# One-plane key pooling, three buffers for the high and low parts, and a new order of work

## The chip, the core and the metric

The kernel runs on one NeuronCore of a Trainium2 chip. Five engines run side by side, each through its own instruction list in order: TensorE (PE, with its weight loads shown as PEld), VectorE (DVE), ScalarE (ACT), GpSimd (POOL) and SyncE (SP), which issues most of the DMA transfers. An instruction that waits holds back everything behind it on its engine. The DMA transfers of all of them run on the same 16 DMA engines. The metric is the time of one execution on the device, in microseconds (us), lower is better.

## What is computed

Attention over keys that are pooled in 4 x 4 blocks, and behind it a soft mixture of experts. q has 4 batches of 12,288 rows of 128; kv is 4 x 384 x 32 x 128, so pooling leaves 768 keys a batch, each the mean of 16 planes of kv.

```
kv_pool = kv.reshape(B, H // 4, 4, W // 4, 4, C).mean(axis=(2, 4))
k = v = kv_pool.reshape(B, -1, C) @ w_sr
s = (q @ k.T) / sqrt(C);  a = softmax(s, -1);  x = a @ v
logits = x @ phi                                   # 32 slots
d = softmax(logits, 0);  slot_input = d.T @ x
slot_out = per expert: relu(slot_input @ w1) @ w2   # 8 experts
out = softmax(logits, 1) @ slot_out
```

## The kernel before, in words

The rows of q are cut into 384 tiles of 128 rows, 96 a batch; 12 tiles make a group, 8 groups a batch, 32 in all. Attention is never written out: what leaves it are the logits of the second stage and running sums over the slots.

For a tile, PE multiplies q by the 768 keys in split precision (lines 388 to 390, six matmuls into `s`), DVE takes the row maximum (394, 395), ACT the exponential into `p` (403). Of each row of `p`, 384 columns are turned on DVE into `pa` (`ptr`, 427). The other 384 go another way: ACT writes their high half in 16 bits, two tiles at a time, into a buffer `hl` (`p_hi`, 410); POOL writes the low half beside it (`p_lo`, 414, one instruction a tile); and SP issues a DMA transpose of the tile from `hl` into `pb` (`p_dma`, 423). There are two `hl` buffers, so a conversion on ACT waits until both transposes of the pair two conversions back have landed. SP issues 384 such transposes, one a tile. SP also loads q for four tiles at a time (234), which ACT and POOL split (368, 372).

Behind every 12 tiles PE makes the group's logits from `pa` (459, `LA`) and `pb` (471, `LB`) in 96 and 36 matmuls; ACT and DVE evacuate one half each (480, 482), PE adds them up (488, `lsel`), DVE turns them into `LL` (497 to 500). A chain over POOL, DVE, PE and ACT (503 to 578) makes the weights `D` of the group, and PE multiplies them with the group's `p` tiles (588, `T`, a pair of tiles is one block of matmuls). POOL and ACT make the row-wise exponentials in `LL` for the last stage (604 to 610).

The pooled keys of the first batch are made on DVE. Those of the next three are pooled by DMA while the batch before runs: `plan_keys` puts a plain load of two planes on SP (257) and seven accumulating loads of two planes on POOL's queue (259), each waiting for the one before, and then one accumulating copy of the first plane onto the second (`kv_fold`, 263). They use idle slots of `LL`. At the switch to the next batch PE forms keys and values from the sum (`pk` 271, `pu` 286, `put` 315, `pv` 331), ACT and DVE evacuate them.

The last stage (the tail) loads w1 and w2 and the spilled `LL` rows (`pb<-spill`, 831), runs the experts (845 to 908), normalises the rows of `LL` on DVE and POOL (949 to 958), and then for each of the 32 groups turns, multiplies, evacuates and stores the result (976 to 995).

The order on PE, DVE, ACT and POOL is written out in advance: every operation gets a key, its place of origin plus an entry of the table `TAU` (raised above the keys of what it depends on), and all are emitted by rising key. SP's list is ordered by the framework.

Of the kernel before, what the change touches and what calls it, by code (L numbers as in the profile page):

```python
# [19 lines left out]
P = 128  # L20
# [35 lines left out]
    "lev0": 18.513, "lev1": 18.513, "crec11": 18.527, "reps": 18.807, "rinv": 18.974, "lsel": 19.037, "ltr": 19.601,  # L56
    "ln": 20.079, "csum19": 20.551, "csum25": 20.707, "mcol": 21.235, "mmm": 21.629, "mred": 22.122, "dsub": 22.358,
# [5 lines left out]
    "kv4": 39.365, "cmul27": 40.126, "bev": 40.196, "uhl": 42.368, "cexp": 43.449, "spill": 44.522, "wl4": 44.887,  # L63
# [32 lines left out]
def attention_then_soft_moe(ctx: ExitStack, tc: tile.TileContext, E, qT, kv0, kvT, w_sr, w_srT, phi, w1, w2, outT, spill):  # L96
# [14 lines left out]
    G = 12  # L111
# [3 lines left out]
    KVC = 2  # L115
    GH = G // 2
    NSL = 16
    NA = 3
# [15 lines left out]
        "s": 3, "T": 1, "x": 1, "p": 13, "pa": 3, "pb": 3, "hl": 2, "q": 3, "qs": 2, "lps": 1, "g": 3,  # L134
# [27 lines left out]
    def kvb(b):  # L162
        o = (b % 2) * (NSL // 2) * G * NS
        return flat[:, o : o + KVC * NK].rearrange("p (a n) -> p a n", a=KVC)

# [88 lines left out]
    def kv_acc(b, c):  # L254
        dst, src = kvb(b), kvT[b - 1, :, c * KVC : (c + 1) * KVC, :]
        if c == 0:
            nc.sync.dma_start(out=dst, in_=src)
        else:
            nc.gpsimd.dma_start(out=dst, in_=src, accum_op=ALU.add, max_dma_last_dim=4 * 2 * NK)

    def kv_fold(b):
        t = kvb(b)
        nc.gpsimd.dma_start(out=t[:, 1:, :], in_=t[:, :1, :], accum_op=ALU.add, max_dma_last_dim=4 * 2 * NK)
        PO[b] = t[:, 1, :]
# [281 lines left out]
    def d_sub(g):  # L546
        d = GD[g]
        d["D"] = ring(gp, "D", [P, G, NS], f"D_{g}", F32, "g")
        nc.gpsimd.tensor_tensor(  # L549
            out=d["D"], in0=lsl(g), in1=MRUN[g].unsqueeze(1).broadcast_to([P, G, NS]), op=ALU.subtract  # L550
        )
# [11 lines left out]
    def d_exp(g):  # L563
        d = GD[g]
        nc.scalar.activation(d["D"], d["D"], AF.Exp)
# [140 lines left out]
    def plan_logits(g):  # L706
# [16 lines left out]
        e1 = op("DVE", "lev1", at, [a], lambda: l_ev(g, 0), use=[sl[0]] + lk)  # L723
        mk = ("x", ("psl", g))
        a = op("PE", "lsel", at, [e0, e1, ops["us", b]], lambda: l_sel(g), acq=[mk], use=lk + [("K", b)])
        ops["lt", g] = op("DVE", "ltr", at, [a] + ([ops["vm", b]] if b and g % GPB == KVC else []), lambda: l_tr(g), acq=[("c", g)], use=[mk, ("g", g)])

    def plan_group(g):
        b = g // GPB
# [322 lines left out]
```

## Time and profile before

| | |
|---|---|
| three timed runs | 1022.58, 1026.76, 1033.25 us; median 1026.76 us |
| profiled execution | 1019.8 us, of which the span of the instructions is 1018.0 us |
| busy share of the span | PE 87%, DVE 77%, ACT 65%, POOL 63% |
| DMA engines | 67.7% for SP's and ACT's transfers, 10.3% for POOL's |
| mean granted TensorE clock | 0.946 of full speed |

Matmuls are pipelined, so a PE that is busy all the time is not necessarily at its peak; instructions that issue a DMA are not counted as busy. A wait is put down to what came last by the profile. In the views below, a stretch is given in us from the start of the span.

### The profile page before, as it was taken

To read this page: it belongs to the slowest core of one execution; us is meant where nothing else is said; L and a number is where in the kernel's file an instruction comes from. 1 tells how busy PE (TensorE), PEld (TensorE's weight loads), DVE (VectorE), ACT (ScalarE), POOL (GpSimd) and SP (SyncE) were. 2 spreads that over 40 slices of the span, in tenths; PEclk is the share of its full clock that TensorE was granted. 3 is DMA by queue.
4 is the path that set the end of the run, shared out by engine and by line. 5 is a ranking of instruction groups with operands and counts; after the bars stand their busy time and mean duration, and the time that the engine had idled before them with its cause. 6 is when DMAs were issued, how large, how long until landed. Compare 5 with 4: busy or idle time off the path is not lost. (4 is left out here: it accounts for less than half of the span.)

```text
span 1018.0 us, 27047 instructions
## 1 busy us (share of the span) xinstructions
PE 884.1 (87%) x10436; PEld 623.3 (61%) x10436; DVE 787.4 (77%) x1496; ACT 663.8 (65%) x1244; POOL 641.1 (63%) x774
## 2 busy tenths in 40 slices
PE   1878999989979999989889989999999999965673
PEld 0756666665756667766666667766777777632341
DVE  6757787877967779878777768978998989935765
ACT  1756767766766678767767758787887888710333
POOL 1556676776657668775766657776776777747300
PEclk9989998999999999999999989999999999987657
DMA  8597886897887898895889886976676676692788
GB/s 325 100 154 135 163 138 133 164 187 134 131 159 143 148 153 150 146 205 119 158 144 151 147 147 129 172 147 108 136 130 113 135 131 125 101 361 120 285 345 361
DMA packets 335264, 168.78 MB, mean 166 GB/s; under 512 B 310432, under 2 KB 312736, under 8 KB 335008
## 3 DMA queue, kind: packets, MB, share of 16 engines
q1 hardware_dynamic: 331248, 149.22, 67.7%
q0 software_dynamic: 3456, 17.70, 10.3%
q8 instruction: 82, 1.34, 0.6%
q14 instruction: 46, 0.38, 0.1%
q10 hardware_dynamic: 432, 0.15, 0.1%
HBM read 62.01 MB, written 28.31 MB: 89 GB/s over the span
## 5 line engine op out<-in xcount | busy, mean ns | idle before, releaser
L414 POOL TENSOR_TENSOR hl<-p,hl 128x384 f16<-128x384 f32 x384 | 349.5, 928 | 205.1 <-ACT hl L410 196.7
L394 DVE TENSOR_REDUCE nm<-s 128x1 f32<-128x768 f32 x384 | 363.3, 946 | 68.9 <-PE s L390 66.4
L403 ACT ACTIVATE p<-s,nm 128x768 f32<-128x768 f32 x384 | 344.0, 896 | 91.3 <-DVE nm L395 83.7
L388 PE MATMUL s<-khi,qhi 128*128 128x384 f32 x768 | 287.6, 374 | 21.8 <-ACT p L403 21.7
L389 PE MATMUL s<-klo,qhi 128*128 128x384 f32 x768 | 263.4, 343 | 2.1 <-DVE klo L278 2.1
L390 PE MATMUL s<-khi,qlo 128*128 128x384 f32 x768 | 263.8, 343 | 0.0
L410 ACT ACTIVATE hl<-p 128x768 f16<-128x768 f32 x192 | 161.2, 840 | 98.9 <-DMA pb<-hl 92.4
L388 PEld LDWEIGHTS s<-khi,qhi 128*128 128x128 f32 x768 | 148.5, 193 | 92.7 <-issue 46.6
L427 DVE STREAM_TRANSPOSE pa<-p 128x768 f32<-128x768 f32 x192 | 182.5, 963 | 0.0
L588 PE MATMUL m<-p,D 128*32 128x192 f32 x3072 | 160.2, 337 | 5.6 <-POOL D L573 4.4
L389 PEld LDWEIGHTS s<-klo,qhi 128*128 128x128 f32 x768 | 149.0, 194 | 3.3 <-DVE klo L278 3.0
L390 PEld LDWEIGHTS s<-khi,qlo 128*128 128x128 f32 x768 | 148.0, 193 | 0.0
L372 POOL TENSOR_TENSOR qlo<-q,qhi 128x512 fp32r<-128x512 f32 x96 | 124.8, 1300 | 25.2 <-ACT qhi L368 25.2
L588 PEld LDWEIGHTS m<-p,D 128*32 128x32 f32 x3072 | 85.9, 111 | 62.4 <-issue 27.3
L459 PE MATMUL lq<-pa,vu 32*32 32x384 f32 x3072 | 88.6, 492 | 1.5 <-DVE pa L427 1.5
L403 ACT ACTIVATION_READ_ACCUMULATOR p<-s,nm 128x1 f32 x384 | 74.1, 193 | 0.0
L395 DVE TENSOR_SCALAR nm<-nm 128x1 f32<-128x1 f32 x384 | 59.1, 154 | 13.2
L459 PEld LDWEIGHTS lq<-pa,vu 32*32 32x32 f32 x3072 | 45.6, 103 | 31.0 <-issue 9.5
L549 POOL TENSOR_TENSOR D<-LL,gm 128x384 f32<-128x384 f32 x32 | 32.4, 1013 | 48.8 <-DVE al L578 41.6
L368 ACT ACTIVATE qhi<-q 128x512 fp32r<-128x512 f32 x96 | 59.6, 621 | 4.6 <-PE s L389 4.6
L471 PE MATMUL lq<-pb,vb 128*32 128x384 f16 x1152 | 53.7, 327 | 7.8 <-DMA pb<-hl 4.4
L982 PE MATMUL po<-ct,sl 32*128 32x384 f32 x192 | 38.3, 738 | 22.9 <-DVE ct L976 22.5
(121 smaller groups left out, 719.5 us busy)
## 6 DMA issues: line engine op xcount, KB each, us to landing
q<-qT SPq DMA_DIRECT2D x96, 256.0 KB, 3.2
outT<-o SPq DMA_DIRECT2D x32, 768.0 KB, 4.5
LL<-kvT POOLq DMA_DIRECT2D x21, 768.0 KB, 8.3
raw<-kv SPq DMA_DIRECT2D x8, 768.0 KB, 9.5
pb<-hl SPq DMA_TRANSPOSE x384, 3.2
w_p<-w SPq DMA_DIRECT2D x6, 768.0 KB, 8.2
pa<-w SPq DMA_DIRECT2D x1, 3328.0 KB, 16.3
spill<-LL SPq DMA_DIRECT2D x16, 192.0 KB, 3.5
```

The source lines that it names most:

```text
L368: nc.scalar.activation(qsp[i][0], src, AF.Copy)
L372: nc.gpsimd.tensor_tensor(out=lo, in0=src, in1=hi.bitcast(F32), op=ALU.subtract)
L388: nc.tensor.matmul(s, hi[:, qc], khi[:, k], start=True, stop=False)
L389: nc.tensor.matmul(s, hi[:, qc], klo[:, k], start=False, stop=False)
L390: nc.tensor.matmul(s, lo[:, qc], khi[:, k], start=False, stop=True)
L394: nc.vector.tensor_reduce(out=NM[t], in_=S[t][:, :, :HK], axis=XY, op=ALU.max, negate=True)
L403: nc.scalar.activation(PP[t // 2][:, t % 2, :].rearrange("p (h n) -> p h n", h=2), S.pop(t)[:, :, :HK], AF.Exp, bias=NM.pop(t), scale=1.0, ...
L410: nc.scalar.activation(HL[k][:, :, 0, :], PP[k][:, :, KA:], AF.Copy)
L414: nc.gpsimd.tensor_tensor(out=hl[:, 1, :], in0=PP[t // 2][:, t % 2, KA:], in1=hl[:, 0, :], op=ALU.subtract)
L427: nc.vector.transpose(out=PA[:, n, :, o : o + 2, :].rearrange("p n a i -> p a n i"), in_=PP[k][:, :, :KA].rearrange("p a (n j) -> p a n j" ...
L459: nc.tensor.matmul(lp(g, c, r), VU[b][rows, kb, :], PA[rows, halves(g), kb, :, :], start=(k == 0), stop=False, skip_group_check=True)
L588: nc.tensor.matmul(d["pst"][c * Q32 : (c + 1) * Q32, :KW], d["D"][:, t, :], pp[:, u, c * KW : (c + 1) * KW], start=(t == 0), stop=(t == G ...
```

## The change

1. The keys are pooled into one plane of 768 columns: one plain load (SP) and fifteen accumulating loads (POOL), of one plane each; the fold is gone. The sum lies in slots 4 and 5 of its half of `LL`, where it lay over slots 0 to 3, and what waits for these slots changes with it.
2. `hl` has three buffers instead of two, q's ring two instead of three, and `D` a ring of its own with two buffers, where it had three.
3. The table `TAU` is new in nearly all its entries, so the order moves on all four engines.

```diff
-    "crec24": -159.684, "crec7": -151.055, "ceps5": -143.302, "hklo1": -137.385, "csum3": -136.384, "hkhi0": -135.084,
+    "cmul8": -199.942, "xo21": -190.996, "csum28": -173.56, "cmul15": -161.438, "hkmm0": -152.436, "hklo1": -144.593,
...
-    KVC = 2
     GH = G // 2
     NSL = 16
+    KVS = 4
...
-        "s": 3, "T": 1, "x": 1, "p": 13, "pa": 3, "pb": 3, "hl": 2, "q": 3, "qs": 2, "lps": 1, "g": 3,
+        "s": 3, "T": 1, "x": 1, "p": 13, "pa": 3, "pb": 3, "hl": 3, "q": 2, "qs": 2, "lps": 1, "g": 3, "D": 2,
...
     def kv_acc(b, c):
-        dst, src = kvb(b), kvT[b - 1, :, c * KVC : (c + 1) * KVC, :]
+        dst, src = kvb(b), kvT[b - 1, :, c, :]
         if c == 0:
             nc.sync.dma_start(out=dst, in_=src)
+            PO[b] = dst
         else:
-            nc.gpsimd.dma_start(out=dst, in_=src, accum_op=ALU.add, max_dma_last_dim=4 * 2 * NK)
-
-    def kv_fold(b):
-        t = kvb(b)
-        nc.gpsimd.dma_start(out=t[:, 1:, :], in_=t[:, :1, :], accum_op=ALU.add, max_dma_last_dim=4 * 2 * NK)
-        PO[b] = t[:, 1, :]
+            nc.gpsimd.dma_start(out=dst, in_=src, accum_op=ALU.add, max_dma_last_dim=4 * NK)
...
-        for c in range(1, R2 // KVC):
+        for c in range(1, R2):
             a = op("POOL", f"kv{c}", t, [a], lambda c=c: kv_acc(nb, c), use=[("kv", nb)])
-        f0 = op("POOL", "kf0", t, [a], lambda: kv_fold(nb), use=[("kv", nb)])
-        kv_ops(nb, t, [[f0], [f0]], [("kv", nb)])
+        kv_ops(nb, t, [[a], [a]], [("kv", nb)])
```

Where the order moves, on ACT, in a group of the second batch (`hl` conversions from `p`, `p` exponentials from `s`; `lps` is the evacuation of the logits behind `LB`). Before, from the group's first conversion shown to the evacuation:

```order
L410 ACTIVATE hl_4831<-p_4765 128x2x384
L403 ACTIVATE p_4817,r_4816<-s_4794,nm_4820 128x768
L403 ACTIVATE p_4860,r_4816<-s_4824,nm_4843 128x768
L410 ACTIVATE hl_4875<-p_4817 128x2x384
L403 ACTIVATE p_4860,r_4816<-s_4833,nm_4856 128x768
L403 ACTIVATE p_4903,r_4816<-s_4862,nm_4885 128x768
L403 ACTIVATE p_4903,r_4816<-s_4878,nm_4898 128x768
L410 ACTIVATE hl_4924<-p_4860 128x2x384
L368 ACTIVATE qhi_4948<-q_4713 128x512
L403 ACTIVATE p_4986,r_4816<-s_4915,nm_4945 128x768
L410 ACTIVATE hl_5003<-p_4903 128x2x384
L480 ACTIVATE lps_4926<-lq_1_4928 128x768
```

and in the change:

```order
L407 ACTIVATE hl_4839<-p_4785 128x2x384
L400 ACTIVATE p_4818,r_4817<-s_4803,nm_4828 128x768
L400 ACTIVATE p_4869,r_4817<-s_4831,nm_4849 128x768
L365 ACTIVATE qhi_4881<-q_4756 128x512
L400 ACTIVATE p_4869,r_4817<-s_4842,nm_4865 128x768
L400 ACTIVATE p_4909,r_4817<-s_4871,nm_4892 128x768
L400 ACTIVATE p_4909,r_4817<-s_4884,nm_4906 128x768
L407 ACTIVATE hl_4932<-p_4818 128x2x384
L566 ACTIVATE da_4861<-da_4861 128x32
L400 ACTIVATE p_4975,r_4817<-s_4911,nm_4934 128x768
L407 ACTIVATE hl_4996<-p_4869 128x2x384
L407 ACTIVATE hl_5023<-p_4909 128x2x384
```

The evacuation stands next behind the last row shown. Before, the last conversion ahead of it writes the buffer of the conversion two earlier, `hl_4875`, seven rows up, which belongs to the next group's first pair; in the change it writes the buffer of the one three earlier, `hl_4839`, the last pair of the group whose logits are evacuated.

On POOL, in the middle of a batch, from the group's row-sum instruction (`r`) on. Before:

```order
L503 TENSOR_SCALAR r_3690<-r_3690 128x12
L414 TENSOR_TENSOR hl_4267<-p_4154,hl_4267 128x384
L372 TENSOR_TENSOR qlo_4318<-q_4110,qhi_4317 128x512
L516 TENSOR_TENSOR LL<-LL,ri_4308 128x384
L414 TENSOR_TENSOR hl_4347<-p_4250,hl_4347 128x384 x2
L549 TENSOR_TENSOR D_4399<-LL,gm_4392 128x384
```

and in the change:

```order
L500 TENSOR_SCALAR r_4063<-r_4063 128x12
L261 DMA LL<-kvT 128x768
L411 TENSOR_TENSOR hl_4562<-p_4447,hl_4562 128x384 x2
L411 TENSOR_TENSOR hl_4626<-p_4499,hl_4626 128x384 x2
L411 TENSOR_TENSOR hl_4653<-p_4539,hl_4653 128x384
L261 DMA LL<-kvT 128x768
L411 TENSOR_TENSOR hl_4653<-p_4539,hl_4653 128x384
L369 TENSOR_TENSOR qlo_4695<-q_4493,qhi_4694 128x512
L513 TENSOR_TENSOR LL<-LL,ri_4682 128x384
L604 TENSOR_TENSOR LL<-LL,RM 128x384
L411 TENSOR_TENSOR hl_4735<-p_4605,hl_4735 128x384 x2
L546 TENSOR_TENSOR D_4783<-LL,gm_4770 128x384
```

Six low halves follow one another behind `r`, and transfers of the keys stand among them. Counted between one `r` and the next, the eight groups of a batch hold 2, 1, 1, 1, 0, 1, 2, 0 of POOL's transfers before (the fold counted) and 0, 1, 3, 3, 3, 1, 2, 2 in the change.

On DVE, at the end of the last group (`acc` is the sum over the group's `T` matmuls, `RM<-pb` the row sums of spilled rows that are being loaded back). Before:

```order
L949 TENSOR_REDUCE RM<-LL 128x12
L949 TENSOR_REDUCE RM<-pb 128x12 x3
L604 TENSOR_REDUCE RM<-LL 128x12
L955 RECIPROCAL RM<-RM 128x12
L949 TENSOR_REDUCE RM<-LL 128x12
L949 TENSOR_REDUCE RM<-pb 128x12
L955 RECIPROCAL RM<-RM 128x12
L578 STREAM_TRANSPOSE al_12149<-da_12096 128x32
L599 SCALAR_TENSOR_TENSOR acc<-acc,al_12149,m 128x192
L626 TENSOR_REDUCE bs_12160<-acc 128x1
```

and in the change:

```order
L575 STREAM_TRANSPOSE al_12148<-da_12116 128x32
L952 RECIPROCAL RM<-RM 128x12 x2
L946 TENSOR_REDUCE RM<-LL 128x12 x2
L952 RECIPROCAL RM<-RM 128x12
L596 SCALAR_TENSOR_TENSOR acc<-acc,al_12148,m 128x192
L623 TENSOR_REDUCE bs_12178<-acc 128x1
L946 TENSOR_REDUCE RM<-pb 128x12 x4
L952 RECIPROCAL RM<-RM 128x12
L654 SCALAR_TENSOR_TENSOR sacc<-sacc,bal_12144,m 128x128
```

The sum `acc` now stands ahead of the reductions that wait for spilled rows; `sacc`, which is next on the way to the experts, stands behind them as before.

## Rows read from the trace of the kernel before

**Rows 1.** The page: the span, and the busy time of each engine.

```profile
span 1018.0 us, 27047 instructions
PE 884.1 (87%) x10436; PEld 623.3 (61%) x10436; DVE 787.4 (77%) x1496; ACT 663.8 (65%) x1244; POOL 641.1 (63%) x774
```

**Rows 2.** Busy time by stretch: length, engines, granted clock, DMA share, GB/s.

```profile
62.52:703.58 641.06, 588.99 (x7199) 421.68 (x7200) 503.61 (x954) 453.85 (x863) 437.90 (x507) 0.98 0.83 148
703.58:875.57 171.99, 170.14 (x2206) 124.44 (x2205) 153.99 (x290) 138.53 (x262) 128.40 (x149) 1.00 0.68 126
875.57:946.56 70.99, 47.17 (x651) 24.84 (x650) 42.68 (x123) 18.46 (x38) 43.77 (x78) 0.86 0.60 196
```

**Rows 3.** The same view, two single groups of the last batch.

```profile
703.58:727.53 23.95, 23.84 (x312) 17.50 (x311) 21.75 (x42) 19.56 (x39) 18.70 (x23) 1.00 0.74 133
803.51:827.72 24.21, 24.10 (x311) 17.49 (x311) 21.51 (x42) 19.53 (x38) 18.32 (x21) 1.00 0.71 132
```

**Rows 4.** Waits (total us, times, longest): three from 62.5:703.6, last from 703.6:875.6.

```profile
ACT hl L410 <- DMA pb<-hl: 85.5, 31, 5.7
PE m L488 <- ACT lps L480: 18.7, 6, 3.5
PE s L388 <- ACT p L403: 17.4, 17, 3.3
ACT hl L410 <- DMA pb<-hl: 2.6, 4, 1.0
```

**Rows 5.** One key transfer: timeline of POOL, SP, ACT, PE; then busy by stretch.

```profile
591.27 0.88 POOL L259 DMA_DIRECT2D LL<-kvT  x1
590.48 8.47 SPq L423 DMA_TRANSPOSE pb<-hl  x4
601.15 0.84 ACT L410 ACTIVATE hl<-p 128x768 f16<-128x768 f32 x1 [5.50 <-DMA pb<-hl]
602.75 1.49 PE L488 MATMUL m<-lps,selb 128*32 128x384 f32 x4 [3.27 <-ACT lps L480]
591.27:603.27 12.00, 8.73 (x170) 4.85 (x160) 6.43 (x11) 5.90 (x13) 5.11 (x8) 0.92 1.02 155
603.27:610.00 6.73, 6.73 (x38) 5.37 (x34) 4.38 (x10) 3.64 (x8) 4.63 (x5) 0.63 0.59 128
```

**Rows 6.** Key transfers: issue on POOL and landing by line 259; page's DMA issues.

```profile
L259 POOL DMA_DIRECT2D LL<-kvT x21: 819/875/1029, 44.9 to 652.4; - x21
DMA to landing us min/median/max: 7.3/8.3/10.1
LL<-kvT POOLq DMA_DIRECT2D x21, 768.0 KB, 8.3
LL<-LL POOLq DMA_DIRECT2D x3, 384.0 KB, 6.0
```

**Rows 7.** DMA queues: POOL's (packets, MB, share of 16 engines' span).

```profile
q0 software_dynamic: 3456, 17.70, 10.3%
```

**Rows 8.** Timeline of PE around the switch to the third batch.

```profile
462.51 0.86 PE L588 MATMUL m<-p,D 128*32 128x192 f32 x16
465.72 0.91 PE L271 MATMUL pk<-LL,w_sb 128*128 128x384 f32 x2
466.47 1.45 PE L286 MATMUL pu<-LL,wp 128*128 128x384 f32 x4
469.27 1.51 PE L588 MATMUL m<-p,D 128*32 128x192 f32 x32
```

**Rows 9.** Timeline of PE and DVE at the end of the last group.

```profile
909.04 5.56 PE L588 MATMUL m<-p,D 128*32 128x192 f32 x96 [1.98 <-POOL D L573]
916.15 1.47 DVE L949 TENSOR_REDUCE RM<-pb 128x12 f32<-128x384 f32 x3 [4.30 <-issue]
920.21 0.41 DVE L599 SCALAR_TENSOR_TENSOR acc<-acc,al,m 128x192 f32<-128x192 f32 x1
920.68 0.66 PE L621 MATMUL m<-ident,acc 128*96 128x128 f32 x2 [6.07 <-DVE acc L599]
```

More of the change, by code (lines that the diff above doesn't have):

```diff
@@ L26 @@
 TAU = {
[29 rows of a table removed]
-    "lev0": 18.513, "lev1": 18.513, "crec11": 18.527, "reps": 18.807, "rinv": 18.974, "lsel": 19.037, "ltr": 19.601,
-    "ln": 20.079, "csum19": 20.551, "csum25": 20.707, "mcol": 21.235, "mmm": 21.629, "mred": 22.122, "dsub": 22.358,
[5 rows of a table removed]
-    "kv4": 39.365, "cmul27": 40.126, "bev": 40.196, "uhl": 42.368, "cexp": 43.449, "spill": 44.522, "wl4": 44.887,
[12 rows of a table removed]
[29 rows of a table added]
+    "mcol": 21.441, "mmm": 21.883, "csum7": 22.133, "mred": 22.329, "dsub": 22.579, "xho12": 22.858, "dexp": 23.18,
[3 rows of a table added]
+    "xho15": 30.893, "bsum": 31.358, "kv3": 31.519, "dal": 31.805, "xh8": 31.827, "umax": 32.854, "csub": 33.213,
[16 rows of a table added]
 }
@@ L162, in kvb @@
     def kvb(b):
-        o = (b % 2) * (NSL // 2) * G * NS
-        return flat[:, o : o + KVC * NK].rearrange("p (a n) -> p a n", a=KVC)
+        o = ((b % 2) * (NSL // 2) + KVS) * G * NS
+        return flat[:, o : o + NK]
     PA = cp.tile([P, 3, KBA, GH, Q32], F32, tag="pa", name="pa")
@@ L547, in d_sub @@
         d = GD[g]
-        d["D"] = ring(gp, "D", [P, G, NS], f"D_{g}", F32, "g")
+        d["D"] = ring(gp, "D", [P, G, NS], f"D_{g}", F32)
         nc.gpsimd.tensor_tensor(
@@ L725, in plan_logits @@
         a = op("PE", "lsel", at, [e0, e1, ops["us", b]], lambda: l_sel(g), acq=[mk], use=lk + [("K", b)])
-        ops["lt", g] = op("DVE", "ltr", at, [a] + ([ops["vm", b]] if b and g % GPB == KVC else []), lambda: l_tr(g), acq=[("c", g)], use=[mk, ("g", g)])
+        ops["lt", g] = op("DVE", "ltr", at, [a] + ([ops["vm", b]] if b and g % GPB == KVS else []), lambda: l_tr(g), acq=[("c", g)], use=[mk, ("g", g)])
     def plan_group(g):
@@ L740, in plan_group @@
         ops["mr", g] = mr
-        sb = op("POOL", "dsub", at, [mr], lambda: d_sub(g), use=gk)
-        ex = op("ACT", "dexp", at, [sb], lambda: d_exp(g), use=gk)
-        a = op("POOL", "dmul", at, [ex, ri], lambda: d_mul(g), use=gk)
+        dk = [("D", g)]
+        sb = op("POOL", "dsub", at, [mr], lambda: d_sub(g), acq=dk, use=gk)
+        ex = op("ACT", "dexp", at, [sb], lambda: d_exp(g), use=gk + dk)
+        a = op("POOL", "dmul", at, [ex, ri], lambda: d_mul(g), use=gk + dk)
         al = a
@@ L751, in plan_group @@
         for pr in range(GP):
-            a = op("PE", f"T{pr}", at, [a], lambda pr=pr: t_mm(g, pr), acq=[mk] if pr == 0 else [], use=[mk, ("p", g * GP + pr)] + gk)
+            a = op("PE", f"T{pr}", at, [a], lambda pr=pr: t_mm(g, pr), acq=[mk] if pr == 0 else [], use=[mk, ("p", g * GP + pr)] + gk + dk)
             ops.setdefault(("T", g), a)
@@ L777, in plan_keys @@
         t = (nb - 1) * TB
-        first = [pool0[0], pool0[1], ops["s", t]] + ([ops["sp", (nb - 2) * GPB + i] for i in range(2 * KVC)] if nb > 1 else [])
+        first = [pool0[0], pool0[1], ops["s", t]] + ([ops["sp", (nb - 2) * GPB + KVS + i] for i in range(2)] if nb > 1 else [])
         a = op("SP", "kv0", t, first, lambda: kv_acc(nb, 0), acq=[("kv", nb)])
-        for c in range(1, R2 // KVC):
+        for c in range(1, R2):
             a = op("POOL", f"kv{c}", t, [a], lambda c=c: kv_acc(nb, c), use=[("kv", nb)])
-        f0 = op("POOL", "kf0", t, [a], lambda: kv_fold(nb), use=[("kv", nb)])
-        kv_ops(nb, t, [[f0], [f0]], [("kv", nb)])
+        kv_ops(nb, t, [[a], [a]], [("kv", nb)])
     for t in range(NT):
```

92 rows, old and new, of the table TAU are left out of this document.

## The prediction, made before the changed kernel was run

> **What bounds the kernel now.** The page's first part names PE as the busiest engine, 884.1 us of 1018.0 [rows 1]. An average says little here, so I cut the span into stretches at the first `LA` matmul of a group: from group 0 to group 23, the time in which keys are pooled by DMA; from group 23 to group 30, in which nothing is pooled; and the tail up to the first store [rows 2]. In the second stretch PE is busy 170.14 of 171.99 us at clock 1.00 and a group takes 23.95 to 24.21 us [rows 3], so there PE is the bound; I take 24.1 us a group. In the first stretch the same work runs 23 times in 641.06 us, and 23 x 24.1 is 554. The three batch switches bring matmuls of their own: `pk` twice 0.91, `pu` 1.45 [rows 8], and I estimate as much again for `put` and `pv`, 6 us a switch, 18 in all. **Some 69 us of the first stretch are lost to something else.** PE's idle time is 641.06 - 588.99 = 52 us of it, and a clock of 0.98 is another 13 [rows 2].
>
> What is lost is read from the waits. ACT's conversions into `hl` wait 85.5 us in the first stretch for transposes to land, and only 2.6 in the second [rows 4]. PE's two large waits, 18.7 us for ACT's evacuation and 17.4 us for exponentials, are for an ACT held up behind such a conversion. One case shows the chain: a key transfer is issued at 591.27; the four transposes on SP's queue take 8.47 us; the next conversion waits 5.50 us; behind it on ACT stands the evacuation, for which PE waits 3.27 us; and in the 6.73 us after that the granted clock is 0.63, so PE runs part of the time at 1.2 instead of 2.4 GHz, 2.5 us more [rows 5]. The DMA engines are full (1.02) during these 12 us. So while keys are pooled, the bound is the DMA engines in bursts, passed on through two `hl` buffers.
>
> **How much a burst is.** POOL's queue takes 10.3% of 1018.0 us for 17.70 MB [rows 1, 7]: 104.9 us, or 4.66 us of all 16 engines for a two-plane transfer and 2.33 for a one-plane one. Without keys a group keeps them busy 0.725 of 24.1 us, 17.5 us [rows 3]. In the 12 us of the case shown, 8.7 + 4.66 = 13.4 are wanted, more than there is; with one plane 8.7 + 2.33 = 11.0, which fits.
>
> **The change, part by part.** The same bytes are moved for the keys, so DMA work is unchanged at 105 us; the transfers become 45 on POOL instead of 24. (a) A third buffer lets a conversion wait for the pair three back. The rows on ACT show what that does just ahead of the evacuation: there the last conversion waited for a pair of the next group, transposed moments ago; now it waits for the last pair of its own group, whose transposes `LB` needs anyway. The 18.7 us of PE waiting for the evacuation have no cause left, nor has the clock lost behind them. (b) A burst is half as long, and the buffer adds room of two tiles, about 4 us at 24.1/12 each.
>
> What remains I bound from both sides. Three groups of a batch hold three transfers each: 17.5 + 3 x 2.33 = 24.5 us of DMA work, and I estimate half a us for the spill of a group, in 24.1. DMA is then the bound by 0.9 us a group, 8 us over nine groups. Above that a transfer costs PE between nothing (it fits) and what it costs now per byte: 69 us over 24 transfers is 2.9, half of it 1.45. I take 0.4, nearer to nothing because both the burst and the room move the right way: 45 x 0.4 = 18. **Left of the 69 us: 26; gained: 43.**
>
> (c) POOL issues 21 more transfers of 0.875 us [rows 6], 18 us; in a group POOL is busy 18.3 to 18.7 of 24.1 us [rows 3], and three issues take 2.6 of the 5.6 that are left, so they are hidden; without that cover they would cost 18. Each transfer also waits on POOL for the one before, and behind it stand the low halves, then transposes, then `LB`. Between two of three in a group lie 18.5 / 3 = 6.2 us of POOL's own work. A one-plane landing is not in the trace. Half of 8.3 is 4.2; the fold, as large, took 6.0; the two-plane median is 8.3 [rows 6]. I take 6.0, the nearest row in size: no wait. From POOL the Trainium skill (DMA: Bandwidth & Descriptors, section "Anatomy of one DMA — SWDGE (gpsimd) path") speaks against cutting transfers: each costs about 2.0 us fixed plus its bytes at 436 GB/s. By it two planes take 3.8 us and one plane 2.9 (an estimate from that page), a cut of a quarter, not a half; the measured 8.3 would become 6.3, and the sum would gain at most a wait of 0.1 us a transfer. The trace's 8.3 for two planes is more than twice the page's 3.8, and the trace decides.
>
> (d) The new table gives PE six blocks of `T` in a group, one more than now: two single ones take 0.86 each, a double one 1.51 [rows 8], so 0.2 us a group, +6 over 30 groups. (e) At a batch switch the double `T` block between `pk` and the first `s`, which covers 1.51 us of waiting for keys [rows 8], moves away: nothing to +4.5 over three switches; I take +2. (f) In the tail `acc` no longer stands behind row sums of spilled rows. `T` ended at 914.6, the row sums started at 916.15, `acc` at 920.21, and PE waited 6.07 us for it [rows 9]. `sacc` still stands behind the row sums, so between 0 and 5.6 us come back; I take -4. (g) The shorter rings for q and `D` I cost at nothing: q is wanted every four tiles, 8 us, and that span hides its load; if loads come late where DMA is full, PE waits for `s` as it does behind a late conversion, which is inside the bounds above. The stores behind the tail run at DMA speed and don't change.
>
> The sum against the profiled execution: 1019.8 - 43 + 6 + 2 - 4 = 981. That execution is 0.7% under the median of the runs (1026.76 / 1019.8 = 1.0068), so on the runs' scale **988 us**, 3.8% below the median.
>
> **Rivals.** *POOL held by its own transfers, in part.* If landing stays at 8.3 us, POOL stands 2.1 us at each of three transfers, 6.3 + 2.6 of issue against 5.6 spare: 3.3 us a group, 30 over nine, in place of the 8. With 0.7 instead of 0.4 a transfer beside it, 62 of the 69 stay lost: 1019.8 - 7 + 4 = 1017, or 1024 on the runs' scale. For it: DMA is full just there, in the groups with three transfers. Against it: the fold's 6.0.
>
> *The loss goes with the bytes.* Then 45 half transfers cost what 24 do now, the 69 us stay, and the change does not do what it says: 1019.8 + 4 = 1024, or 1031. For it: DMA work is the same. Against it: the case shown overflows by 1.4 us only because 4.66 come at once.
>
> *Slower: the chain of landings is POOL's pace.* The same place as the first rival, with a longer landing. With landing L, a group of three loses 3 x (L - 6.2) + 2.6 - 5.6; nine of them outweigh the 69 us from L = 9.8 on. At 10.5, beyond the longest two-plane landing of 10.1 [rows 6], it is 9.9 us a group, 89 in all: 1019.8 + 20 + 4 = 1044, or 1051. For it: 45 landings in series beside transposes that fill the engines. Against it: half the bytes would have to land later than the whole does now.
>
> **How the numbers follow.** Forecast 0.68, POOL held in part 0.11, loss with the bytes 0.11, slower 0.10. The likeliest case has its own range: 0 to 0.75 us a transfer leaves 8 to 42 us, 963 to 997 and so 969 to 1004 on the runs' scale. For the whole, the low end takes all 69 us back and the tail's 5.6 without (e): 951, or 958. The high end, 1028, holds the first rival and nearly half of the second, and leaves out the rest, about 0.17. A measurement of this kernel can tell about 1% from no change, so faster means under 1016: the forecast and a quarter of the first rival, 0.70; within 1% the rest of that one and most of the second, 0.19; slower 0.11.
>
> **What would show it.** In the changed profile: from the first `LA` to that of group 23 about 600 us instead of 641, at clock 0.99 or more and a DMA share near 0.9; ACT's wait for transposes in that stretch under 30 us; PE's wait for the evacuation under 5; a landing of one plane between 4.2 and 6.3; POOL not idle in front of its own key transfers; `btr`'s wait at the end of the last group under 2 us. The forecast is wrong if `LB` on PE waits for transposes by more than 20 us in all (the wait only moved), if landing exceeds 8 us, or if groups without key transfers take longer than 24.5 us, which would be the new order's own doing.

## The result, and the profile after

The changed kernel takes 975.76 us in the median (971.75 to 982.60, four runs) against 1028.51 us for the kernel before on the same chip: 0.950 of it, 95% interval 0.942 to 0.957. Measured once more beside the experiments it stood at 0.956 (0.950 to 0.963). The forecast was 988 us, 3.8% below; it is 4.4 to 5.0%.

Its profiled execution took 982.6 us, the slowest of its four, and the profiled one of before, 1019.8, lies 0.8% below that kernel's median here. So the two traces differ by 37.2 us of span, where the medians differ by 52.8. The page's span and busy times, answering [rows 1]:

```profile
span 980.8 us, 27134 instructions
PE 873.0 (89%) x10436; PEld 618.0 (63%) x10436; DVE 788.5 (80%) x1496; ACT 661.3 (67%) x1244; POOL 659.9 (67%) x795
```

Busy time by stretch, as in [rows 2]: `LA` of group 0 to group 23, to group 30, and to the first store (length, then PE, PEld, DVE, ACT, POOL busy; granted clock, DMA share, GB/s):

```profile
61.93:669.43 607.50, 577.03 (x7199) 416.26 (x7199) 505.74 (x954) 452.83 (x862) 459.46 (x530) 0.99 0.93 157
669.43:841.51 172.08, 171.40 (x2208) 124.45 (x2204) 152.52 (x289) 137.27 (x263) 128.56 (x150) 1.00 0.70 127
841.51:909.54 68.03, 48.57 (x654) 25.35 (x650) 44.76 (x125) 18.45 (x37) 42.63 (x76) 0.82 0.63 206
```

The first stretch gives 641.06 - 607.50 = 33.6 of the 37.2 us: PE is idle 30.5 us in it instead of 52.1, and the same 7199 matmuls take 577.0 instead of 589.0. The second stretch is unchanged, and the tail up to the first store gives 70.99 - 68.03 = 3.0. The other 15.6 us of the medians' difference are in neither of the two traces.

Waits of the whole span (total us, times, longest), for [rows 4], first those of the kernel before, with which the runs below are compared:

```profile
ACT hl L410 <- DMA pb<-hl: 92.4, 39, 5.7
PE s L388 <- ACT p L403: 21.7, 21, 3.3
PE lq L471 <- DMA pb<-hl: 4.4, 4, 1.7
PE m L588 <- POOL D L573: 4.4, 3, 2.0
SPq L234 <- POOL qlo L372: 22.2, 6, 11.3
```

and those of the changed kernel, with its key transfers on POOL, for [rows 6, 7]:

```profile
ACT hl L407 <- DMA pb<-hl: 25.1, 15, 3.4
PE lq L468 <- DMA pb<-hl: 8.6, 5, 2.2
PE s L385 <- ACT p L400: 7.3, 9, 1.7
POOL LL L261 <- DMA LL<-kvT: 13.3, 13, 2.1
L261 POOL DMA_DIRECT2D LL<-kvT x45: 846/883/1188, 77.1 to 641.4; - x45
DMA to landing us min/median/max: 5.1/6.1/9.7
q0 software_dynamic: 6480, 17.70, 12.0%
```

ACT's conversions wait 25.1 us for transposes (92.4 before), PE's wait of 18.7 us for ACT's evacuation is gone from the list, and its wait for exponentials has fallen from 21.7 to 7.3. `LB`, to which the wait could have moved, waits 8.6 (4.4 before). One plane lands after 6.1 us.

So far nearly all of it reads as forecast; that POOL waits for its own transfers, 13.3 us, was not. But this trace holds three edits at once, and can't say which of them did it.

### The profile page after: what moved, and what is told of

Read it like the earlier page. It is cut to its first block, busy times and chain, and to the rows that moved or that the text cites. A ratio compares the mean times of both kernels' runs of the same rounds, so it can differ in the third digit from the quotient of the medians.

```text
span 980.8 us, 27134 instructions
## 1 busy us (share of the span) xinstructions
PE 873.0 (89%) x10436; PEld 618.0 (63%) x10436; DVE 788.5 (80%) x1496; ACT 661.3 (67%) x1244; POOL 659.9 (67%) x795
## 3 DMA queue, kind: packets, MB, share of 16 engines
q0 software_dynamic: 6480, 17.70, 12.0%
## 5 line engine op out<-in xcount | busy, mean ns | idle before, releaser
L411 POOL TENSOR_TENSOR hl<-p,hl 128x384 f16<-128x384 f32 x384 | 353.3, 962 | 97.1 <-issue 52.5
L385 PE MATMUL s<-khi,qhi 128*128 128x384 f32 x768 | 284.3, 370 | 7.3 <-ACT p L400 7.3
L424 DVE STREAM_TRANSPOSE pa<-p 128x768 f32<-128x768 f32 x192 | 179.3, 958 | 0.0
L407 ACT ACTIVATE hl<-p 128x768 f16<-128x768 f32 x192 | 158.1, 836 | 29.5 <-DMA pb<-hl 25.1
L585 PE MATMUL m<-p,D 128*32 128x192 f32 x3072 | 168.0, 340 | 6.8 <-POOL D L570 4.4
L369 POOL TENSOR_TENSOR qlo<-q,qhi 128x512 fp32r<-128x512 f32 x96 | 132.4, 1379 | 56.6 <-ACT qhi L365 55.5
L585 PEld LDWEIGHTS m<-p,D 128*32 128x32 f32 x3072 | 82.9, 111 | 67.0 <-issue 30.2
L392 DVE TENSOR_SCALAR nm<-nm 128x1 f32<-128x1 f32 x384 | 59.1, 154 | 13.2
L479 DVE COPY lps<-lq 128x768 f32<-128x768 f32 x32 | 30.6, 958 | 47.8 <-PE lq L468 47.8
L456 PEld LDWEIGHTS lq<-pa,vu 32*32 32x32 f32 x3072 | 45.5, 103 | 32.5 <-issue 14.0
L979 PE MATMUL po<-ct,sl 32*128 32x384 f32 x192 | 38.7, 739 | 24.5 <-DVE ct L973 24.1
## 6 DMA issues: line engine op xcount, KB each, us to landing
raw<-kv SPq DMA_DIRECT2D x8, 768.0 KB, 11.6
```

The lines of the kernel that those rows point to most:

```text
L369: nc.gpsimd.tensor_tensor(out=lo, in0=src, in1=hi.bitcast(F32), op=ALU.subtract)
L385: nc.tensor.matmul(s, hi[:, qc], khi[:, k], start=True, stop=False)
L407: nc.scalar.activation(HL[k][:, :, 0, :], PP[k][:, :, KA:], AF.Copy)
L411: nc.gpsimd.tensor_tensor(out=hl[:, 1, :], in0=PP[t // 2][:, t % 2, KA:], in1=hl[:, 0, :], op=ALU.subtract)
L424: nc.vector.transpose(out=PA[:, n, :, o : o + 2, :].rearrange("p n a i -> p a n i"), in_=PP[k][:, :, :KA].rearrange("p a (n j) -> p a n j" ...
L456: nc.tensor.matmul(lp(g, c, r), VU[b][rows, kb, :], PA[rows, halves(g), kb, :, :], start=(k == 0), stop=False, skip_group_check=True)
```

## The experiments

The prediction gave 43 us to the third `hl` buffer and the shorter transfers together. Before the experiments I split them: 32 for the buffer (18.7 us of waiting and 13 of clock) and 11 for the transfers; the new order had a cost of 8 and a gain of 4 in the tail. So each of the three is taken out, and put in, by itself.

**Take one part out of the changed kernel.** First the changed kernel again, as a mark.

> The changed kernel once more, as the common mark for the three kernels beside it. It stands at 0.950 of the kernel before (0.942 to 0.957). Its profiled execution shown so far, 982.6 us, is the slowest of its four. If that is chance, a second profile lies near the median of 976 and the 7 us are missing in the first stretch, from group 0's LA to group 23's, 600 us instead of 607.5. If the slow place is built into the order, the first stretch is 607 again.

Measured: 978.02 us, 0.956 (0.950 to 0.963). Its profiled execution took 984.3 us, again the slowest of its runs, but the first stretch isn't what makes it slow (point (f) below has what does):

```profile
60.64:663.67 603.03, 574.50 (x7200) 414.38 (x7200) 505.64 (x954) 452.57 (x862) 459.43 (x530) 0.99 0.94 158
```

603.0 lies between the 600 and the 607 of the expectation, so neither of its two cases is shown; two executions of one kernel differ by 4.5 us in this stretch.

> The changed kernel with two buffers for high and low parts instead of three, nothing else. My theory (the third buffer is the larger part: it takes away the 18.7 us for which PE waited for the evacuation and the 13 us of clock, 32 of the 43): 0.950 + 32/1028 = 0.981 of the kernel before; ACT's conversions wait for landings by 60 us or more in the span, instead of 25. Rival A (the short transfers carry the gain, the third buffer has little to do once a burst is 2.33 us long): within 0.01 of the changed kernel, 0.950 to 0.960, and ACT's wait stays under 40. Rival B (the new order carries the gain): under 0.960 too.

```diff
-"p": 13, "pa": 3, "pb": 3, "hl": 3, "q": 2,
+"p": 13, "pa": 3, "pb": 3, "hl": 2, "q": 2,
```

Measured: 1112.88 us, 1.090 (1.086 to 1.095). No theory had this: without the third buffer the new order is 9% slower than the kernel before. Waits of the span, and rows from the timeline of ACT in a group in which no keys are pooled (start, length, instruction, idle before it):

```profile
ACT hl L407 <- DMA pb<-hl: 158.3, 60, 5.9
PE s L385 <- ACT lps L477: 86.9, 31, 5.4
814.93 0.84 ACT L407 ACTIVATE hl<-p 128x768 f16<-128x768 f32 x1
817.24 0.83 ACT L407 ACTIVATE hl<-p 128x768 f16<-128x768 f32 x1
822.04 0.84 ACT L407 ACTIVATE hl<-p 128x768 f16<-128x768 f32 x1 [3.97 <-DMA pb<-hl]
822.79 0.79 ACT L477 ACTIVATE lps<-lq 128x768 f32<-128x768 f32 x1
```

The new order puts three conversions of the next group ahead of the evacuation. With two buffers the third of them, at 822.04, needs the buffer of the first, written at 814.93; ACT stands 3.97 us, the evacuation behind it is late, and PE waits for it 31 times in the 32 groups. The new order is written for three buffers.

> The changed kernel with the keys pooled as before by two-plane transfers and a fold: each two-plane transfer stands where the first of its two one-plane transfers stood, the fold where the last stood; three buffers and the new order otherwise kept. My theory (halving the burst is the smaller part, 11 of the 43 us): 0.950 + 11/1028 = 0.961 of the kernel before, with ACT's wait for landings between 30 and 50 us. Rival A (the short transfers carry the gain): 0.980 or more, with ACT's wait above 60. Rival B (the new order carries the gain): 0.950 to 0.955.

```diff
-dst, src = kvb(b), kvT[b - 1, :, c, :]
+dst, src = kvb(b), kvT[b - 1, :, c * KVC : (c + 1) * KVC, :]
...
-        for c in range(1, R2):
+        for c in range(1, R2 // KVC):
...
+        f0 = op("POOL", "kf0", t, [a], lambda: kv_fold(nb), use=[("kv", nb)])
```

Measured: 1001.54 us, 0.979 (0.974 to 0.985). In the new order two-plane transfers cost 0.979 - 0.956 = 0.023, 23 us; for this order my 11 was too small. Rival A's 0.980 lies inside the interval, but the wait of ACT's conversions, 35.5 us, is in my range of 30 to 50 and not above its 60. The waits:

```profile
PE lq L474 <- DMA pb<-hl: 25.2, 8, 5.5
ACT hl L413 <- DMA pb<-hl: 35.5, 18, 5.7
```

`LB` waits 25.2 us where it waits 8.6 in the changed kernel, up to 5.5 at once. The places of the two-plane transfers were my choice; better ones may cost less.

> The kernel before with the new table of places alone: two buffers, two-plane transfers and a fold at the places described for the run with two planes. My theory (the order itself brings only the shorter wait at the end, 4 us, and costs 8 at the sixth block of T and the batch switch): 1.00 to 1.01 of the kernel before, ACT's wait for landings 70 us or more. Rival B (the order carries the gain, by transfers and spills standing where DMA is free): 0.96 to 0.975, with ACT's wait halved.

Only the table is exchanged, with the transfers' entries of the run above. Measured: 1145.3 us, 1.123 (1.117 to 1.130), with the waits of the run with two buffers:

```profile
ACT hl L412 <- DMA pb<-hl: 192.9, 54, 7.2
PE s L390 <- ACT lps L482: 81.4, 29, 5.2
```

**Put one part into the kernel before.** The new order brings nothing without the buffer. Does the buffer without the order?

> The kernel before with three buffers for high and low parts, and the shorter rings for q and D that make room for them; old order, two-plane transfers. Theory C (the buffer takes away ACT's waits in any order, as my sum had it: 18.7 us of PE's wait for the evacuation and the 13 us of clock): 1 - 32/1028 = 0.969 of the kernel before, ACT's wait for landings under 35 us. Theory D (buffer and order are one piece: the old order places few conversions where a third buffer helps, the new one is written for it): 0.985 to 1.00, ACT's wait above 60.

```diff
-"hl": 2, "q": 3, "qs": 2, "lps": 1, "g": 3,
+"hl": 3, "q": 2, "qs": 2, "lps": 1, "g": 3, "D": 2,
```

Measured: 1061.15 us, 1.036 (1.030 to 1.042), slower than before, which neither theory allowed. Its waits:

```profile
ACT hl L410 <- DMA pb<-hl: 5.8, 5, 2.2
ACT qhi L368 <- DMA q<-qT: 114.7, 28, 9.8
PE s L388 <- ACT p L403: 83.5, 43, 8.5
SPq L234 <- POOL qlo L372: 80.6, 36, 11.3
```

The buffer did what was expected of it: the conversions wait 5.8 us instead of 92.4 in the span of before. But ACT now waits 114.7 us for loads of q. SP's queue stands in front of such a load 36 times, 80.6 us, until POOL has read the buffer of two loads earlier (6 times, 22.2 us, before). That is the ring of q, which I had costed at nothing. The next run leaves it and the ring of `D` alone.

> The kernel before with a third buffer for high and low parts and nothing else: the rings for q and D keep their length (there is room for that), old order, two-plane transfers. The run with the short q ring took ACT's wait for landings from 92 to 5.8 us, and put a wait of 114.7 us for loads of q in its place. Theory C (the buffer gives what the sum says, and the short ring of q took it away and more): about 0.969 of the kernel before, at most 0.975, ACT's conversions wait under 15 us and its q conversions under 15. Theory D (the old order can't use the buffer; the queue of transposes is what holds): 0.99 or more, and the wait is found at another place, LB on PE or the q conversions.

```diff
-"p": 13, "pa": 3, "pb": 3, "hl": 2, "q": 3,
+"p": 13, "pa": 3, "pb": 3, "hl": 3, "q": 3,
```

Measured: 973.66 us, **0.954 (0.946 to 0.962)**. One digit gives the whole gain of the change, more than theory C's 0.969; ACT's conversions wait 16.0 us, just above theory C's 15. Stretches and waits:

```profile
60.18:655.75 595.57, 569.89 (x7199) 412.66 (x7199) 504.49 (x954) 457.71 (x863) 438.27 (x507) 0.99 0.91 160
655.75:827.49 171.74, 170.24 (x2205) 124.37 (x2204) 153.39 (x290) 138.45 (x263) 128.31 (x149) 1.00 0.68 127
ACT hl L410 <- DMA pb<-hl: 16.0, 10, 5.4
PE s L388 <- ACT p L403: 2.7, 10, 0.5
PE lq L471 <- DMA pb<-hl: 17.6, 6, 6.7
```

The first stretch falls from 641.06 to 595.57, 45.5 us: 26.4 of it are PE's idle time (52.1 to 25.7) and 19.1 its busy time. The granted clock accounts for about 7 of the 19.1: at 0.98 it costs 12.8 of 641 us, at 0.99 6.0 of 596. `lsel`, the block of matmuls that waits for the evacuation, is busy 11.0 us less (some of it at the lower clock, so the two overlap). The same stretch for `lsel` alone, before and here:

```profile
62.52:703.58 641.06, 31.52 (x184) 5.44 (x184) 0.98 0.83 148
60.18:655.75 595.57, 20.50 (x184) 3.71 (x184) 0.99 0.91 160
```

PE's wait for the evacuation isn't in the list any more, that for exponentials is 2.7 us (21.7 before); `LB` waits more, 17.6 against 4.4. Against the run with the short rings, 1.036, the two rings of q and `D` cost 0.082, 84 us; the trace puts the wait at q's.

**The transfers in the old order**, with two buffers, with three and the short rings, and with three and long rings:

> The kernel before with one-plane transfers: the first of each two where the two-plane transfer stood, the second halfway to the next, the last where the fold stood; old order, two buffers. Theory C (half the burst saves PE what the sum had for it, 11 us): 0.985 to 0.99. Theory D (in the new order one-plane transfers were worth 0.979 - 0.956 = 0.023, that is 23 us, and the burst is the same in any order): 0.97 to 0.98. Rival (the loss goes with the bytes): 1.00.

```diff
-        for c in range(1, R2 // KVC):
+        for c in range(1, R2):
```

> The kernel before with three buffers and one-plane transfers at the places of the run with one plane; old order elsewhere. Theory C (buffer and transfers are the whole gain): 0.950 to 0.960, as the changed kernel. Theory D (the new order is a third of it): 0.965 to 0.980.

```diff
-"hl": 2, "q": 3, "qs": 2, "lps": 1, "g": 3,
+"hl": 3, "q": 2, "qs": 2, "lps": 1, "g": 3, "D": 2,
...
-        for c in range(1, R2 // KVC):
+        for c in range(1, R2):
```

> The kernel before with a third buffer and with one-plane transfers, the rings for q and D as before, old order. What the changed kernel has over this run is what the new order is worth with both parts at hand. Theory C: 0.950 to 0.960, the order is worth nothing by itself. Theory D: 0.975 or more, the order is worth at least half of the gain. Rival on the transfers (in the old order one-plane transfers bring nothing, 0.999 with two buffers): the same as the run with the third buffer only, within 0.005.

```diff
-"p": 13, "pa": 3, "pb": 3, "hl": 2, "q": 3,
+"p": 13, "pa": 3, "pb": 3, "hl": 3, "q": 3,
...
-        for c in range(1, R2 // KVC):
+        for c in range(1, R2):
```

Measured: 1025.95 us, 0.999 (0.994 to 1.004), with two buffers; 1038.14 us, 1.014 (1.007 to 1.020), with three and the short rings; 969.88 us, 0.953 (0.946 to 0.960), with three and the long rings. With short rings neither theory had allowed 1.014. So where q's ring is long, halving the transfers changes nothing, 0.999 against 1 and 0.953 against 0.954; where it is short, it is worth 1.036 - 1.014 = 0.023 (from the unrounded ratios), as much as in the new order. Waits of the run with two buffers, and of the one with three buffers and long rings:

```profile
PE m L492 <- ACT lps L484: 8.4, 5, 2.2
PE s L392 <- ACT p L407: 25.4, 25, 4.4
PE m L592 <- POOL D L577: 17.4, 6, 7.3
POOL LL L268 <- DMA LL<-kvT: 16.3, 2, 8.9
```

```profile
ACT hl L414 <- DMA pb<-hl: 3.7, 5, 1.9
PE lq L475 <- DMA pb<-hl: 6.0, 4, 4.3
PE m L592 <- POOL D L577: 18.4, 8, 7.3
POOL LL L268 <- DMA LL<-kvT: 17.0, 3, 8.9
q0 software_dynamic: 6480, 17.70, 12.3%
```

With two buffers PE's wait for the evacuation falls from 18.7 to 8.4 us, as half the burst should do, and `T` pays for it: 17.4 us for weights from POOL (4.4 before), which stands up to 8.9 us in front of its own next transfer. With three buffers the shorter transfers take `LB`'s wait from 17.6 to 6.0 and ACT's from 16.0 to 3.7, POOL waits 17.0 us for them, `T` waits 18.4 for weights, and the first stretch is 596.90 instead of 595.57.

This isn't a test of the burst alone. With the one-plane transfers the sum moves to slots 4 and 5 of `LL`, which are spilled later than slots 0 to 3, while the first transfer on POOL keeps its early place in the old order. In the run with three buffers and long rings the keys of the third batch begin like this:

```profile
242.07 0.37 SPq L617 DMA_DIRECT2D spill<-LL  x1
245.16 0.33 SPq L265 DMA_DIRECT2D LL<-kvT  x1
249.81 0.91 POOL L268 DMA_DIRECT2D LL<-kvT  x1 [8.86 <-DMA LL<-kvT]
255.17 1.51 PE L592 MATMUL m<-p,D 128*32 128x192 f32 x16 [7.27 <-POOL D L577]
```

The plain load follows the spill, POOL stands 8.86 us until it has landed, and `D`, behind it on POOL, keeps PE waiting 7.27 us. At the fourth batch the same costs PE 5.8, so 13.0 of the 18.4 us come from the place of the sum and not from the length of a transfer. What shorter transfers are worth in the old order without that isn't shown, nor why the gain appears with short rings alone.

**What pooling still costs, and two tries at less.**

> The changed kernel without its 45 key transfers on POOL; the first plane alone is loaded, so that 15 of 16 planes are missing from the keys of three batches and its output isn't the reference's. It shows what pooling by DMA still costs in the changed kernel. My sum leaves 26 us of loss in the first stretch: the time falls by 26 to about 0.930 of the kernel before. Rival (what is left there is not the keys', but the order's own and the batch switches'): it falls by less than 10 us, to 0.945 or more.

```diff
-        for c in range(1, R2):
+        for c in range(1, 1):
             a = op("POOL", f"kv{c}", t, [a], lambda c=c: kv_acc(nb, c), use=[("kv", nb)])
```

Measured: 955.92 us, 0.931 (0.924 to 0.938), 0.025 below the changed kernel measured again and 0.019 below its first measurement, 19 to 26 us. Its first stretch, and ACT's wait for transposes in the span:

```profile
58.28:639.63 581.35, 570.74 (x7199) 412.31 (x7200) 505.14 (x954) 453.27 (x862) 420.72 (x485) 0.99 0.73 134
ACT hl L407 <- DMA pb<-hl: 1.0, 2, 0.6
```

581.35 is 26.2 us less than the 607.50 of the changed kernel's first trace and 21.7 less than the 603.03 of its second; the sum had left 26. ACT's conversions wait 1.0 us for transposes in this run (25.1 with the key transfers), so it is these that make them late.

> The changed kernel with its fifteen one-plane transfers of a batch at equal distances of 4.76 tiles between the first and the last, instead of three in each of three groups: 2 or 3 a group. Without transfers the changed kernel is 20 us faster. If that loss is DMA being full in groups of three (17.5 + 7.0 us wanted of 24.1), spreading takes a third of it back: 6 us, 0.950 against 0.956 for the changed kernel. If it goes with the number of transfers, no change.

```diff
-    "kv2": 28.045, "kv3": 31.519, "kv4": 36.485,
+    "kv2": 29.668, "kv3": 34.425, "kv4": 39.183,
```

The others follow at the same distance up to `kv15`, which stays.

Measured: 973.27 us, 0.954 (0.947 to 0.961), against 0.956: a third of the loss, 6 us, is inside the interval, so this is not decided by the time. The trace shows nothing given back: its first stretch is 606.1 us, against 607.5 and 603.0.

> As the even run, and begun earlier: the last exponentials and the spill of a group stand 18 tiles sooner, so that the keys' buffer is free and the fifteen transfers spread from tile 8 to tile 91 of a batch, 5.97 tiles or 12 us apart, two a group. If the loss is DMA being full, two a group want 17.5 + 4.7 + 0.5 = 22.7 of 24.1 us and half of the 20 us come back: 0.945. If the exponentials, being earlier, hold up ACT ahead of PE's evacuations, it is slower than the even run.

```diff
-    "kv1": 24.91, "kv2": 28.045, "cexp": 55.114, "spill": 57.583,
+    "kv1": 8.0, "kv2": 13.966, "cexp": 36.5, "spill": 38.9,
```

Measured: 1005.43 us, 0.979 (0.968 to 0.989), 2.5% above the even run. `LB` waits 25.3 us in its trace (7.8 in the even run's), and no wait of PE for the evacuation is in the list, so the expectation's reason for a loss isn't what shows. Two things are moved at once here, the exponentials with their spill and the transfers, and which of them costs it stays open. None of the versions is shown to beat the changed kernel; before with the third buffer and one-plane transfers (969.88) lies lowest, within the uncertainty. Before with the third buffer and the tail order of the change wasn't tried.

## Why the prediction was right, point by point

**The bound was read rightly.** Key transfers keep the DMA engines full in bursts, transposes land late, a conversion on ACT stands in front of the evacuation, and PE waits and then runs part of the time at 1.2 GHz. Without key transfers ACT's wait for transposes is 1.0 us; with them and one buffer more, and nothing else, it is 16.0 instead of 92.4. One row was misread: the 8.47 us of [rows 5] are the time in which SP issued the four transposes, one after the other, not the time that they took.

**(a) was mis-sized, and it is the whole gain.** I gave the buffer 18.7 + 13 = 32 us of the first stretch; alone it gives 45.5 there (0.046 of the time, 47 us). The step that failed is what I counted to it. I had said that both waits of PE, 18.7 for the evacuation and 17.4 for exponentials [rows 4], come from an ACT held up by a conversion, and then gave the buffer only the first and its clock. It takes the first whole and most of the second (21.7 to 2.7 in the span), and 11.0 us in which `lsel` counted as busy; of the 13 of clock only about 7 come back, and `LB` takes 13.2. The terms don't add up to the 45.5; a few us lie in small waits that aren't followed here. I also tied the effect to the new order's rows. The old order has it too: with a third buffer its last conversion ahead of the evacuation, `hl_5003`, needs `hl_4831`, three back, which is the last pair of the group whose logits are evacuated.

**(b) The shorter burst, 11 us: 0 in the old order as built.** There the waits for transposes do fall, by 11.6 us at `LB`, and PE's wait for `D` takes more than that back (18.4 us against 3.3), 13.0 of it from the later plain load. So it isn't shown that a shorter burst has nothing to give beside a third buffer; that the buffer had taken most of the loss already is shown, by its 45.5 us. The 23 us that one-plane transfers are worth in the new order don't make a gain over the kernel before: they only take back what that order loses with two-plane ones, 0.979 against 0.954 for the old order with three buffers.

**What is left, 26 us: 22 to 26 by the traces without and with key transfers.** The floor under it was a little low: 23 x 24.1 + 18, and 5 to 7 for (d) and (e), is 577 to 579 us, and the run without transfers takes 581.35. I had read 24.1 from two quiet groups; the seven of [rows 2] take 171.99 us, 24.6 each. The make-up of the 22 to 26 isn't settled: 8 of it was a floor from groups of three transfers, and spreading them did not give that back beyond the uncertainty.

**(c) right in the landing, not in the wait.** 6.1 us measured, 6.0 taken. POOL does wait for its own transfers, 13.3 us in all, at most 2.1 at once. By the two medians (8.3 for two planes, 6.1 for one) a cut by half in bytes shortens a landing by 27%. The rule of the Trainium skill (DMA: Bandwidth & Descriptors, section "Anatomy of one DMA — SWDGE (gpsimd) path") gives, as an estimate, a cut from 3.8 to 2.9 us, 24%: the trace agrees in the share, and its times are twice as long.

**(d) was cancelled, (e) fits.** In the second stretch PE is busy 171.40 instead of 170.14 us, 0.18 a group, near the 0.2 of the sixth `T` block; but PE's idle time there falls from 1.85 to 0.68, and the stretch is as long as before: +6 in the sum, about 0 measured. The switch groups of the run without transfers take 31.6, 31.6 and 30.0 us from `LA` to `LA`, 20.9 over three times 24.1, where the sum had 18 + 2; the old order without transfers wasn't run, so what the move itself costs isn't shown.

**(f) right in size.** PE waits 0.55 us for `acc` instead of 6.07, and from `LA` of group 30 to the first store it is 68.0 us instead of 71.0: 3.0, forecast 4. Five more traces in the new order, all with three buffers, have 67.4 to 69.2 there; the old order with the third buffer alone has 72.0, though PE waits only 2.6 us for `acc` in it, so that wait alone isn't shown to be the gain. What did not hold is that nothing changes behind the first store: the same instructions take 66.7 us at a granted clock of 0.83 in the even run and 77.6 at 0.52 in the repeat of the changed kernel, more than any term of the sum but the first. Timeline of DVE and PE, answering [rows 9]:

```profile
878.17 5.77 PE L585 MATMUL m<-p,D 128*32 128x192 f32 x96 [1.35 <-POOL D L570]
884.02 0.41 DVE L596 SCALAR_TENSOR_TENSOR acc<-acc,al,m 128x192 f32<-128x192 f32 x1
884.49 0.42 PE L618 MATMUL m<-ident,acc 128*96 128x128 f32 x2 [0.55 <-DVE acc L596]
```

**(g) was wrong as a rule.** In the new order no cost of the short rings is seen: ACT's q conversions don't wait for DMA there (that order with long rings wasn't run). In the old one they cost 84 us. My cover for it, "q is wanted every four tiles, 8 us, and that span hides its load", looked at the load alone and not at SP's queue, in which the load stands until its buffer is free. There was no need to shorten them in the old order: with three buffers, the longer rings fit as well.

**Rivals.** POOL held by its own transfers is real, 13 to 17 us of waiting. In the changed kernel PE's wait for `D` is 4.4 us, as before, so it does not decide the total there; in the old order it takes back what the short burst gives. The loss going with the bytes meets the number in the old order (0.999), but not by its reason: one wait of PE fell there and another rose. With the third buffer it fails, as the same bytes cost much less. A longer landing did not come.

So the mechanism was right and the split of the 43 us wrong, one term too small and the other, of the same sign, too large; that they met in the total is partly luck. By the sum the first stretch is 641 - 43, and 5 to 7 more for (d) and (e), so 603 to 605 us and not the 600 that I named; it came out at 607.5 and 603.0. The median lies 12 us under the forecast, and neither trace shows where. The change as a whole is worth what its third buffer alone is worth.

## What to carry to other kernels

Before several edits are priced, find the one wait that they all work on and price that once: a ring one buffer longer took most of the wait, of what stood behind it and half of the clock, and the halved bursts added nothing that could be measured. Look also at what else an edit moves: with the shorter transfers the sum changed its slots, and in the old order that cost as much as they saved. A buffer that is taken from another ring has its price on the queue that refills that ring, and an order that was written for one ring length says nothing about another: here the same order was 4.4% faster with three buffers and 9% slower with two. Put such an edit into the old kernel alone first; it was one digit.

## What the hardware showed that was not expected

The same 17.70 MB of keys keep the DMA engines longer in halves: with three buffers and long rings, 10.6% of 973.7 us, 103 us, in two-plane transfers and 12.3% of 974.4, 120 us, in one-plane ones; I had taken the work as unchanged at 105. The packets are 6480 instead of 3456. The total of the two runs is the same. The row for the two-plane run:

```profile
q0 software_dynamic: 3456, 17.70, 10.6%
```
